# Other priorities for the list schedule of a routed two-part feed-forward stage

## The chip, the core and the metric

The kernel runs on one core of a Trainium2 chip. The metric is the device time of one execution in microseconds (us); lower is better. Times "before" are three runs of the kernel, and one further execution was profiled.

## The reference, cut to what matters

Attention with a feature map comes first, then a routing that gives every one of 8 experts 576 of the 4608 tokens, then two matrix products per expert, then a third and a fourth product that all tokens share:

```
def _moe_ref(x, w_gate, w1, w2):
    ...
    for e in range(E):                        # E = 8, 576 tokens each
        mask = assigned == e
        h = np.maximum(x[mask] @ w1[e], 0.0)  # 512 -> 1024
        out[mask] = h @ w2[e]                 # 1024 -> 512
    ...
def _moe2_ref(x, w_in, w_out):
    h = x @ w_in                              # 512 -> 2048
    g = h - np.tanh(h)
    return (g @ w_out)                        # 2048 -> 512
```

Tokens are assigned greedily: the expert that fills next is found by counting, so the routing of expert p+1 needs the result of expert p.

## The kernel before, in words

The kernel has two parts. `attention` is the first and lasts about a third of the time. `ffn` is the second, and only its order is at stake here. Float32 products are made of three float16 products (high times high, high times low, low times high), so each operand has a high and a low half.

**The planner.** Each part records its operations in a `Sched` object: engine, an estimated duration, what is read and written, and a priority (a smaller number goes first). `run` then plays the engines forward with the estimated durations. Whenever an engine comes free it takes, of the operations whose inputs are ready at that moment, the one with the smallest priority; it waits for nothing that isn't ready unless that is far more urgent. What comes out is one fixed order of instructions for each engine. On the chip every engine works through its order strictly, and waits at an instruction whose inputs are late.

```
            while pend[e] and pend[e][0][0] <= t:
                i = heapq.heappop(pend[e])[1]
                heapq.heappush(avail[e], (self.ops[i][4], i))
```

**The stages of one expert p**, with `TE[p] = 136 p` as the base of its priorities:

- `xt(p)`: five gathers of token rows (GpSimd, L1161), a scaled high half (ScalarE, L1179), a low half (VectorE, L1180), and a transposing DMA on SyncE's queue (L1183). The row buffers `xg` are two, the half buffers `xs` one, so the five rounds follow one another. Priority `TE[p] - 30`.
- `wprep(p)`: gathers of the expert's w1 and w2 (GpSimd, L1097), squares for a norm (ScalarE, L309), high halves (ScalarE, L1118) and low halves (VectorE, L1119). For w1 the priority is `TBT[p-1] + w1`, for w2 `TBT[p-1] + w2`, with `TBT[p] = TE[p] + tb`.
- `g1(p)` and `g2(p)`: 16 and 8 groups of matmuls with 288 columns (L1190, into `mm`), three PSUM banks. After each group of g1 come a relu (ScalarE, L1203, tile `r`), a high half (ScalarE, L1204) and a low half (GpSimd, L1205, tile `xh`); after each group of g2 a high half (L1216) and a low half (VectorE, L1217, tile `gw`).
- `scale_g(p)`: norms of the result (L1233, L1237) and a scale.
- `batch(p)`: 512 of the expert's tokens through the third and fourth product in 16 tiles f. A tile is 12 matmuls of 512 columns into an `mm` bank (L1190), five ScalarE and five VectorE operations for h - tanh(h) (L1315 to L1336, the last two the halves of `gw`), and 12 matmuls of 512 columns that add to four `po` banks (L1342). Up to five tiles of `gw` can stand finished. At the end each `po` bank is copied out (ScalarE, L1353) and scattered to the output rows (GpSimd, L1357). `batch(8)` does the same for the 64 remaining tokens of all experts.
- `routing(p+1)`: sixteen counting steps (VectorE L898, ScalarE L896, a count column on VectorE L846, a small matmul L902 into `rtp`, a comparison on VectorE L904), then the list of rows (L981, L988, `idx` at L992). Priority `TE[p] + route`; its matmuls have at most priority 0, which puts them ahead of nearly all others. The planner treats them as ready `late` us later than their inputs (for p over 0).

The priorities inside `batch`, all from the table `FT`:

```
            for f in range(16):
                tf = T0 + FT["step"] * f
                S.pri = tf
...
                S.pri = tf + FT["sq"]
...
                S.pri = tf + FT["dv"]
...
                S.pri = tf + FT["dv2"]
...
            S.pri = T0 + FT["step"] * 16 + FT["ev"]
```

Here `T0` is `TBT[p]`. The first product of tile f has `tf`; square, tanh and the two functions after the square have `tf` plus `sq`, `th`, `sq2`; the four VectorE steps `dv` and `dv2`; the halves `gh`; the fourth product `lag`; the copies out `ev`. The entry `h` is read nowhere.

Of the kernel before, what the change touches and what calls it, by code (L numbers as in the profile page):

```python
# [38 lines left out]
NW = 96  # L39
MS = 2.0 ** -12  # L40

FT = {'expert': 136.0, 'step': 5.3, 'lag': 11.0, 'route': 5.0, 'xt': -30.0, 'g1': 3.0, 'g2': 24.0, 'g2s': 6.0, 'sg': 49.0, 'tb': 50.0, 'w1': 30.0, 'w2': 40.0, 'rest': 10.0, 'ev': 8.0, 'tb8': 85.0, 'sq': 1.0, 'th': 1.2, 'sq2': 1.1, 'dv': 1.0, 'dv2': 2.0, 'gh': 3.0, 'h': 0.0, 'late': 1.2, 'room': 0.0}
AT = {'hd': -201.4, 'lag': 3.4, 'prep': -30.4, 'load': 19.8, 'proj': -53.9, 'expk': -22.7, 'sub': -13.1, 'expq': -137.2, 'kv': 2.1, 'num': -13.8, 'div': -82.9, 'fin': -101.4, 'conv': 81.9, 'hi': -25.5, 'lo': 83.2, 'tr': 27.2, 'vp': -0.0, 'qproj': 40.6, 'max': 11.5, 'mt': -5.3, 'sqx': -36.8, 'gate': 32.2, 'land': 2.6, 'room': 0.0}
CW = 512
XPE = {0}
# [236 lines left out]
class Kernel:  # L282
# [535 lines left out]
    def routing(self, p, after=()):  # L818
# [33 lines left out]

        late = 1e3 * FT["late"] if p else 0.0

# [164 lines left out]
    def ffn(self):  # L1019
# [3 lines left out]
        pps = ctx.enter_context(tc.tile_pool(name="psf", bufs=1, space=PSUM))  # L1023
        S = self.S = Sched(tc, ports=True, room=1e3 * FT["room"])
        v, act, gp = nc.vector, nc.scalar.activation, nc.gpsimd
# [39 lines left out]

        TE = [FT["expert"] * p for p in range(E)]
        TBT = [t + FT["tb"] for t in TE]
        TBT.append(TBT[-1] + FT["tb8"])

# [12 lines left out]
        def wprep(p, *pri):  # L1082
# [3 lines left out]
            for n, wf in enumerate((w1f, w2f)):  # L1086
# [6 lines left out]
                for c in range(4):  # L1093
                    for b in range(1 + n):
# [10 lines left out]
                S.pe(60, lambda sb=sb: nc.tensor.matmul(self.rtp[:, 508:512], self.onesb, sb, start=False, stop=True, skip_group_check=True), [kss + str(c) for c in range(4)], ["norm"],  # L1105
                     room=1e3 * FT["late"] if p else 0.0)
                S.dve(4, lambda ss=ss: v.tensor_reduce(ss[:, 6:7], self.rtp[:, 508:512], axis=AX.X, op=OP.add), ["norm"], [kss])
# [305 lines left out]
```

## Time and profile before

| | us |
|---|---|
| three runs: median (lowest to highest) | 1783.58 (1779.04 to 1784.16) |
| the profiled execution | 1777.59 |
| its span, first to last instruction | 1775.8 |
| TensorE busy | 1638.1 (92%) |
| VectorE, ScalarE, GpSimd busy | 1333.1, 1270.8, 515.9 |

PE is TensorE's matmuls, PEld its weight loads, DVE VectorE, ACT ScalarE, POOL GpSimd, SP SyncE. A granted clock of 1.00 is 2.4 GHz and 0.50 is 1.2 GHz; a value between is a mean over a stretch at both. The second part has its first expert matmul at 566 us and its last matmul ends at 1758 us.

### The profile page before, as it was taken

What the parts mean: (1) busy time and instruction counts of PE and PEld (TensorE: products, weight loads), DVE (VectorE), ACT (ScalarE), POOL (GpSimd) and SP (SyncE); (2) the same over time, 40 slices, a digit from 0 to 9 for tenths busy, and PEclk for the clock granted to TensorE, in tenths of its full rate; (3) what the DMA queues carried; (4) which work ended last, traced back from release to release, by engine and by line L of the source; (5) the groups of instructions that cost most, each with busy time, mean ns of one, the idle gap of its engine ahead of it and who ended that gap; (6) DMA issues with size and microseconds to landing.
All of it is one profiled execution on the core that took longest, in us unless ns stands there. A gap on an engine that the chain in (4) does not pass through costs nothing. (4 is left out here: it accounts for less than half of the span.)

```text
span 1775.8 us, 32280 instructions
## 1 busy us (share of the span) xinstructions
PE 1638.1 (92%) x11448; PEld 1066.1 (60%) x11448; DVE 1333.1 (75%) x4118; ACT 1270.8 (72%) x2513; POOL 515.9 (29%) x559
## 2 busy tenths in 40 slices
PE   6899999999935999999999999999999999999995
PEld 5888888888822744754754654664664664564442
DVE  6778888778878499589589689689679548436784
ACT  7787889877775679678678668668758658546653
POOL 3332245423043434432332332322322430210000
PEclk9999999889966999999999999999999999999998
DMA  8778776765503022022022022022113250000000
GB/s 202 171 183 190 185 168 153 160 169 142 140 19 115 11 84 63 28 84 69 25 84 65 25 79 71 28 67 76 32 61 83 63 107 13 25 1 1 18 7 24
DMA packets 230419, 145.95 MB, mean 82 GB/s; under 512 B 166080, under 2 KB 208960, under 8 KB 230256
## 3 DMA queue, kind: packets, MB, share of 16 engines
q1 hardware_dynamic: 214208, 90.25, 22.3%
q0 software_dynamic: 16048, 53.62, 9.4%
q8 instruction: 90, 1.47, 0.3%
q14 instruction: 73, 0.60, 0.1%
HBM read 89.16 MB, written 18.87 MB: 61 GB/s over the span
## 5 line engine op out<-in xcount | busy, mean ns | idle before, releaser
L1342 PE MATMUL po<-wout,gw 128*128 128x512 f16 x1728 | 401.3, 380 | 7.6 <-DVE gw L1336 3.9
L1190 PE MATMUL mm<-xh,wt 128*128 128x288 f16 x3072 | 392.2, 288 | 17.2 <-ACT r L1203 10.9
L1190 PE MATMUL mm<-gw,win 128*128 128x512 f16 x1728 | 397.2, 379 | 5.5 <-DVE gw L1217 3.0
L1190 PEld LDWEIGHTS <-wt 128*128 128x128 f16 x3072 | 296.1, 99 | 103.1 <-issue 17.4
L1342 PEld LDWEIGHTS <-gw 128*128 128x128 f16 x1728 | 164.3, 98 | 205.4 <-DVE gw L1336 11.4
L1190 PEld LDWEIGHTS <-win 128*128 128x128 f16 x1728 | 166.0, 98 | 199.3 <-issue 8.2
L1097 POOL DMA_INDIRECT wt<-moe_w,wrow x96 | 125.8, 1310 | 288.9 <-issue 148.4
L544 PE MATMUL bKV<-vp,kp 128*128 128x96 f32 (+1 forms) x1152 | 173.6, 290 | 3.6 <-ACT kvs L551 3.6
L570 PE MATMUL bN<-kvs,qt 128*128 128x96 f32 (+1 forms) x1152 | 158.1, 285 | 5.1 <-ACT qt L527 3.1
L1205 POOL TENSOR_TENSOR xh<-r,xh 128x288 f16<-128x288 f32 x128 | 95.7, 758 | 215.2 <-ACT xh L1204 214.1
L544 PEld LDWEIGHTS bKV<-vp,kp 128*128 128x128 f32 x1152 | 148.2, 197 | 12.9 <-POOL vp L450 4.2
L570 PEld LDWEIGHTS bN<-kvs,qt 128*128 128x128 f32 x1152 | 144.9, 198 | 8.3 <-ACT qt L527 3.3
L1335 ACT ACTIVATE gw<-s,sc 128x512 f16<-128x512 f32 x128 | 91.9, 718 | 53.4 <-DVE s L1328 46.3
L1315 ACT ACTIVATE u<-mm,sc 128x512 f32<-128x512 f32 x128 | 87.0, 679 | 58.4 <-PE mm L1190 57.4
L1336 DVE SCALAR_TENSOR_TENSOR gw<-s,sc,gw 128x512 f16<-128x512 f32 x128 | 98.1, 766 | 18.9 <-ACT gw L1335 18.4
L1324 DVE SCALAR_TENSOR_TENSOR u<-mm,sc,u 128x512 f32<-128x512 f32 x128 | 94.5, 741 | 20.2 <-ACT t L1316 17.2
L1328 DVE COPY_PREDICATED s<-mk,t 128x512 f32<-128x512 uint16 x144 | 105.5, 733 | 0.9
L1317 ACT ACTIVATE s<-u,cst 128x512 f32<-128x512 f32 x144 | 102.9, 714 | 1.3 <-DVE gw L1336 1.2
L1318 ACT ACTIVATE mk<-u,cst 128x512 f16<-128x512 f32 x144 | 102.4, 711 | 0.0
L1327 DVE SCALAR_TENSOR_TENSOR s<-s,u 128x512 f32<-128x512 f32 x144 | 99.9, 694 | 0.8
L904 DVE TENSOR_SCALAR_CACHE_REDUCE r_nn<-rtp,r_rem 128x7 f32<-128x7 f32 x112 | 24.9, 223 | 96.6 <-PE rtp L902 96.5
L1325 DVE SCALAR_TENSOR_TENSOR t<-mm,sc,t 128x512 f32<-128x512 f32 x128 | 94.7, 740 | 2.5 <-ACT t L1316 2.4
(312 smaller groups left out, 2905.6 us busy)
## 6 DMA issues: line engine op xcount, KB each, us to landing
rawk<-k SPq DMA_DIRECT2D x32, 256.0 KB, 3.5
rawv<-v SPq DMA_DIRECT2D x32, 256.0 KB, 3.5
gw<-moe_w_in SPq DMA_DIRECT2D x32, 256.0 KB, 3.2
gw<-moe_w_out SPq DMA_DIRECT2D x32, 256.0 KB, 3.1
rawq<-q SPq DMA_DIRECT2D x30, 256.0 KB, 3.9
xd<-X SPq DMA_DIRECT2D x32, 192.0 KB, 2.6
xd<-X SPq DMA_DIRECT2D x32, 64.0 KB, 2.4
wt<-moe_w,wrow POOLq DMA_INDIRECT x96, 4.2
```

Source lines behind the costliest of these rows:

```text
L544: mm(o, kp[:, c, a * NF:(a + 1) * NF], r, start=sl == 0 and a == 0, stop=sl == 8 and a == 1, skip_group_check=True)
L570: mm(o, qt[:, a, c], r, start=a == 0, stop=a == 1, skip_group_check=True)
L1097: S.pool(1040, lambda dst=dst, col=col, wf=wf: gp.indirect_dma_start(out=dst, out_offset=None, in_=wf, in_offset=bass.IndirectOffsetOnAxis ...
L1190: nc.tensor.matmul(pt.t[:, 0:un], wt(a, d), xs[hl][:, d, u0:u0 + un], start=d == 0 and a == 0 and hl == 0, stop=d == nb - 1 and a == 1)
L1205: S.pool(700, lambda r=r, f=f, u0=u0, un=un: gp.tensor_tensor(hl[:, f, u0:u0 + un], r, hh[:, f, u0:u0 + un], OP.subtract), [kr, f"h.{f}h{u ...
L1317: S.act(512, lambda u=u, s_=s_: act(s_, u, AF.Square, bias=cst[:, 0:1], scale=PC ** 0.5), [ku, "pa"], [ks], pri=tf + FT["sq2"])
L1318: S.act(512, lambda u=u, mk=mk: act(mk, u, AF.Relu, bias=cst[:, 8:9], scale=1024.0), [ku, "t2"], [km], pri=tf + FT["sq2"])
L1325: S.dve_s(512, lambda t=t, pt=pt, sc=sc: v.scalar_tensor_tensor(t, pt.t, sc[:, 0:1], t, op0=OP.mult, op1=OP.subtract), [pt, ksc, kt], [kt])
L1327: S.dve(512, lambda s_=s_, u=u: v.scalar_tensor_tensor(s_, s_, PC * PB, u, op0=OP.add, op1=OP.mult), [ks, ku], [ks], port=True)
L1328: S.dve(512, lambda s_=s_, mk=mk, t=t: v.copy_predicated(s_, mk.bitcast(U16), t), [ks, km, kt], [ks], port=True)
L1336: S.dve_s(512, lambda s_=s_, g=g, sc=sc: v.scalar_tensor_tensor(g[:, 1], s_, sc[:, 2:3], g[:, 0], op0=OP.mult, op1=OP.subtract), [ks, kgr ...
L1342: nc.tensor.matmul(outs[t].t, g[:, a, 128 * t:128 * t + 128], self.wout[:, w, f, :], start=f == 0 and k_ == 0, stop=f == 15 and k_ == 2)
```

## The change

Sixteen numbers of the table `FT` are replaced, fifteen of which are read. No operation is added, removed or altered, and no estimated duration either; only the planner's order of the second part comes out otherwise.

```
-FT = {'expert': 136.0, 'step': 5.3, 'lag': 11.0, 'route': 5.0, 'xt': -30.0, 'g1': 3.0, 'g2': 24.0, 'g2s': 6.0, 'sg': 49.0, 'tb': 50.0, 'w1': 30.0, 'w2': 40.0, 'rest': 10.0, 'ev': 8.0, 'tb8': 85.0, 'sq': 1.0, 'th': 1.2, 'sq2': 1.1, 'dv': 1.0, 'dv2': 2.0, 'gh': 3.0, 'h': 0.0, 'late': 1.2, 'room': 0.0}
+FT = {'expert': 136.0, 'step': 1.8, 'lag': 12.4, 'route': 5.0, 'xt': -30.0, 'g1': 2.5, 'g2': 21.1, 'g2s': 5.2, 'sg': 46.4, 'tb': 53.6, 'w1': 30.0, 'w2': 40.0, 'rest': 27.4, 'ev': -1.8, 'tb8': 64.6, 'sq': 1.0, 'th': 25.4, 'sq2': 3.4, 'dv': 20.9, 'dv2': 2.0, 'gh': 3.4, 'h': -3.3, 'late': 0.6, 'room': 0.0}
```

## Rows read from the trace of the kernel before

**Rows 1.** The page: span, TensorE's busy share, granted clock in 40 slices.

```profile
span 1775.8 us, 32280 instructions
...
PE 1638.1 (92%) x11448; PEld 1066.1 (60%) x11448; DVE 1333.1 (75%) x4118; ACT 1270.8 (72%) x2513; POOL 515.9 (29%) x559
...
PEclk9999999889966999999999999999999999999998
```

**Rows 2.** Busy us of each engine in stretches of 20 us (instructions), clock, DMA.

```profile
940.00:960.00 20.00, 20.00 (x94) 9.11 (x93) 20.00 (x31) 17.67 (x28) 6.48 (x5) 1.00 0.33 79
...
1020.00:1040.00 20.00, 19.11 (x158) 14.84 (x157) 11.92 (x62) 8.40 (x22) 0.00 (x0) 1.00 0.00 1
...
1740.00:1760.00 20.00, 15.72 (x70) 6.30 (x68) 13.29 (x20) 8.31 (x14) 0.97 (x1) 1.00 0.04 14
```

**Rows 3.** What TensorE waited for, 600 to 1760 us: total, times, longest.

```profile
PE mm L1190 <- ACT r L1203: 6.6, 9, 2.0
PE mm L1190 <- DVE gw L1217: 5.4, 7, 2.4
PE po L1342 <- DVE gw L1336: 3.9, 8, 1.5
PE po L1342 <- ACT gw L1332: 2.2, 2, 1.7
PE mm L1190 <- DVE u L1324: 2.0, 1, 2.0
...
PE po L1342 <- ACT gw L1353: 0.6, 1, 0.6
...
PE po L1342 <- ACT gw L1335: 0.5, 2, 0.3
PE mm L1190 <- DVE t L1325: 0.5, 1, 0.5
PE rtp L902 <- DVE r_cnt L846: 0.4, 1, 0.4
```

**Rows 4.** The columns of rows 2, two stretches of 4 us.

```profile
708.00:712.00 4.00, 3.56 (x17) 1.87 (x16) 4.00 (x6) 4.00 (x7) 2.19 (x2) 0.72 0.16 28
...
1440.00:1444.00 4.00, 4.00 (x21) 2.60 (x20) 0.75 (x2) 2.34 (x6) 0.00 (x0) 0.58 0.44 98
```

**Rows 5.** VectorE's groups during one batch, 902 to 988 us: busy us, mean ns.

```profile
L1119 DVE SCALAR_TENSOR_TENSOR wt<-wt,sc 128x1024 f16<-128x1024 f32 x8 | 10.2, 1276 | 0.0
L1180 DVE SCALAR_TENSOR_TENSOR xs<-xg,cst,xs 128x512 f16<-128x512 f32 (+1 forms) x5 | 3.7, 738 | 0.0
```

**Rows 6.** Timeline of routing (start, us, [idle before <- releaser]), three places.

```profile
934.80 1.18 POOL L1161 DMA_INDIRECT xg<-xd,idx  x1 [8.48 <-DVE idx L992]
...
1021.25 0.15 DVE L846 TENSOR_SCALAR r_cnt<-r_ac 128x1 f16<-128x1 f32 x1
...
1023.00 0.17 PE L902 MATMUL rtp<-r_cnt,c 128*128 128x7 f16 x1
...
1274.46 0.17 PE L902 MATMUL rtp<-r_cnt,c 128*128 128x7 f16 x1 [0.45 <-DVE r_cnt L846]
```

**Rows 7.** Timeline of the conversions of token rows, two places.

```profile
973.91 0.74 DVE L1180 SCALAR_TENSOR_TENSOR xs<-xg,cst,xs 64x512 f16<-64x512 f32 x1
...
1437.24 0.72 ACT L1179 ACTIVATE xs<-xg,cst 128x512 f16<-128x512 f32 x1 [4.98 <-DMA xh<-xs]
```

**Rows 8.** Timeline after the last scatter of batch 7.

```profile
1550.02 0.97 POOL L1357 DMA_INDIRECT out<-gw,idx  x1 [2.50 <-DMA out<-gw,idx]
...
1551.78 0.41 ACT L1203 ACTIVATE r<-mm 128x288 f32<-128x288 f32 x1 [3.43 <-POOL xh L1205]
...
1552.24 2.04 PE L1190 MATMUL mm<-xh,wt 128*128 128x288 f16 x12 [1.99 <-ACT r L1203]
```

**Rows 9.** Timeline of TensorE's last matmuls.

```profile
1755.16 3.06 PE L1342 MATMUL po<-wout,gw 128*128 128x512 f16 x12 [1.74 <-ACT gw L1332]
```

## The prediction

> **What bounds the kernel now.** I read the page first, then the stretches of 20 us over the second part, then TensorE's waits, and only then single places in the timeline. TensorE is busy for 92% of the span [rows 1], but the page cannot say whether a busy TensorE is at its peak. The stretches can: in the middle of a batch 94 matmuls pass in 20 us, 0.213 us each [rows 2], and 512 columns at 2.4 GHz are 512/2.4 = 0.213 us. There the array has no hidden room. So TensorE bounds the second part, its work is fixed by the instructions, and a new order can only win back waits, clock lost after waits, and something at the end. The nine waits shown sum to 6.6 + 5.4 + 3.9 + 2.2 + 2.0 + 0.6 + 0.5 + 0.5 + 0.4 = 22.1 us [rows 3]. To them come stretches in which the granted clock fell: 0.72 for 4 us and 0.58 for 4 us, each after a wait [rows 4]. At 0.58 of full speed 4 us do 2.3 us of work, so 1.7 us are lost; at 0.72 it is 1.1 us. The room is thus about 25 us, 1.4% of the time, and a gain beyond it is excluded for the part after 600 us. Before that only `g1`'s own step and `late` differ, and I cost the ramp at nothing: its cover is that routing 0 and the first weights keep their priorities. If ramp orders shift anyway, I allow 2 us either way.
>
> VectorE is the second engine to watch: full, 20.00 of 20, in mid-batch, but 11.92 of 20 while the next expert's second product runs [rows 2]. TensorE is then starved at the end of a batch not because there is too much VectorE work in a cycle, but because too much of it falls into the batch.
>
> **The change part by part.**
>
> *Batch against preparation.* Before, the operations of tile f sit at 5.3 f, so from the sixth tile on the w1 conversion (30) outranks them, from the eighth w2 (40), and from the eleventh the token rows (`TE[p+1]` - 30, which is 56 behind `T0`). Now the first product, square, both functions and the halves lie at 1.8 f to 1.8 f + 3.4, ahead of nearly all preparation; tanh (1.8 f + 25.4) and `dv` (1.8 f + 20.9) fall behind w1 from tiles 3 and 6, behind w2 from tiles 9 and 11, and never behind the token rows (52.4, against at most 52.4). Since each tile needs `dv`, w1 keeps about its place, w2 moves back by two or three tiles, the token rows to the end or into gaps. That is 10.2/2 = 5.1 us of w2 work and 3.7 us of token work [rows 5] that stand less in the way of the late tiles. The waits it aims at are those of batch ends: 3.9 + 2.0 + 0.5 + 0.5 = 6.9 us [rows 3] and 1.1 us of clock [rows 4]. Bounds: 0, if the total of VectorE's work before the batch's end stays what it is, and 8.0 if all go. I take 5 us, nearer to all, because of the next part.
>
> *`late` from 1.2 to 0.6.* Each counting step has one matmul that the planner now places 0.6 us earlier. One step shows it: the count ends at 1021.40 and the matmul starts at 1023.00, 1.60 us later [rows 6]. Sixteen steps would end 16 x 0.6 = 10 us sooner, and so would the list and the first gather, now at 934.80, 32 us into the batch [rows 6]. VectorE's list work then falls partly into the half-empty stretch before the batch, and the token rows start earlier. The gain is counted above. The price: of 1.60 us, 1.0 is left, and where it is less than 0.6 TensorE waits. This happens today once, for 0.45 us [rows 6]; in all 0.4 us [rows 3]. Bounds over seven routings of 16 steps: 0, and 7 x 16 x 0.6 = 67 us if every step lost the whole 0.6. By the shown step nearly all cost nothing; I take 2 us of loss.
>
> The Trainium skill (TensorE: Matmul & The Clock Gate, Part 3, The mechanism) says that matmuls start and end strictly in program order, while only weight loads are pulled ahead. By that rule a routing matmul placed too early holds up every matmul behind it, and its shortfall is paid in full; the upper bound just given is what the sum would rise by. The row of 1274.46 agrees, its wait being TensorE idle time; no row shows more than one such wait.
>
> *First product before fourth.* Before, fourth products (`lag` 11.0) alternate with first ones from tile f - 2; now all first products outrank them (12.4 is 6.9 tiles), so TensorE runs ahead as far as three banks allow. Inside a batch this costs nothing: TensorE has the other product to do, and up to five finished tiles can wait. If that cover went, a batch would lose one bank's turn, a 2.6 us tile. In the last batch it pays: the last tile starts sooner, while fourth products are still in hand, and the wait of 1.74 us before the last twelve matmuls [rows 9], one of 2.2 us in all [rows 3], shrinks. Bounds 0 and 2.2; I take 1.5. The chain of scatters behind is not altered.
>
> *Copies out (`ev`) and the mixed batch.* They move ahead of the mixed batch's first tiles, which removes the 0.6 us [rows 3]; taken as 0.5.
>
> *g1, g2, sg, rest.* Their spacing shrinks, but inside these stages nearly nothing competes. The waits for the first product of a batch (5.4 us, seven times [rows 3]) are six of about half a us, the path from the last group's bank through ScalarE and VectorE, and I leave those. The seventh, 2.4 us, follows a ScalarE instruction that stood 4.98 us waiting for a transposing DMA [rows 7] with a copy-out of g2 behind it, and 1.7 us of clock were lost after it [rows 4]: 4.1 us that hang on where the token rows stand in ScalarE's order. Bounds 0 and 4.1; taken as 2.
>
> *What stays.* The 6.6 us behind relus [rows 3]. In the place shown, GpSimd waits 2.50 us at the fourth scatter for the third one's landing, the subtraction of g1 queues behind it, the relu waits 3.43 us for a free tile and TensorE 1.99 us [rows 8]. No priority here shortens a landing.
>
> **Sum.** -5 + 2 - 1.5 - 0.5 - 2 = -7 us; in the profile's own time 1777.6 - 7 = 1770.6 us. That execution is 6.0 us below the median of the three, so against the median the forecast is 1783.6 - 7 = 1776.6 us, rounded to 1776.5.
>
> **The rivals.**
>
> *A: the waits move but do not go.* VectorE does the same work per cycle, and if routing ends no sooner on the chip, the batch still ends with VectorE full; the first five us fall away. The sum is then +2 - 1.5 - 0.5 - 2 = -2: 1781.5 us. For it: VectorE full at 20.00. Against: 8 us idle in the stretch before [rows 2]. That the new order is nearly the old one ends at the same time.
>
> *B: slower, through the routing matmuls.* If the lead time in the plan is used up by real delays, half of the 112 steps may lose 0.3 us: 17 us instead of 2, and the sum is -7 + 15 = +8: 1791.5 us. It decides from a mean loss of (7 + 2)/112 = 0.08 us per step on. For it: the one wait of 0.45 us. Against: 1.60 us in the shown step.
>
> *C: the scatter waits go too,* because copies out come at other moments against g1: a further -6.6, and with it 1770 us. Nothing in the rows speaks for it but that their times depend on the order.
>
> A late last token row is no rival of weight: the last of five is converted at 973.91 [rows 7], about 15 us before the batch's fourth products end, and only half of each g1 group needs the last two.
>
> **How the numbers follow.** A measurement of this kernel tells about 0.3%, 5.4 us, from no change; the three runs span 5.1 us (the table above). Forecast 0.48 (own range -3 to -14 us; 0.39 of it beyond 5.4), A 0.27 (0.25 within, 0.02 faster), B 0.18 (0.15 slower, 0.03 within), C 0.07 (faster). Faster 0.48, same 0.37, slower 0.15. The range reaches from the room nearly used up, 1783.6 - 19 = 1765, to somewhat short of B, 1789; beyond lie some 0.08 on either side.
>
> **What would show it.** Right: fewer waits for `gw` and `u` at batch ends, first gathers about 10 us earlier in the batch, VectorE below 20.00 late in the batch, a shorter wait before the last twelve matmuls, relu waits as before. Wrong: waits at L902 and L988 of several us (B), or the list of waits with the same 20 us under other lines (A), or a preparation that is late, with g1 waiting for `xh` or `wt`.

## The result, and the profile after

The changed kernel takes 1794.40 us (median of 4 runs, 1790.94 to 1797.47) against 1782.92 us of the kernel before (4 runs): a ratio of 1.0062, 95% interval 1.0034 to 1.0089. It is slower, by about 11 us, where 7 us of gain were forecast. The profiled execution took 1790.94 us.

The page and the stretches of 20 us of the changed kernel, with the columns of [rows 1] and [rows 2]:

```profile
span 1789.2 us, 32383 instructions
...
PE 1638.3 (92%) x11448; PEld 1065.8 (60%) x11448; DVE 1333.1 (75%) x4118; ACT 1264.9 (71%) x2513; POOL 486.4 (27%) x559
...
PEclk8999999889966999999999999999999999999998
```

```profile
960.00:980.00 20.00, 20.00 (x96) 9.04 (x95) 18.54 (x44) 14.97 (x27) 0.90 (x1) 1.00 0.19 38
980.00:1000.00 20.00, 20.00 (x117) 10.64 (x116) 13.98 (x69) 7.40 (x17) 1.01 (x1) 1.00 0.05 17
1000.00:1020.00 20.00, 14.56 (x117) 10.96 (x115) 8.06 (x29) 13.12 (x33) 11.10 (x14) 1.00 0.10 41
```

TensorE's busy time is the same to 0.2 us, so the 13.4 us of longer span are waiting. The batch itself has become what the change aims at: TensorE 20.00 of 20 to its end, with VectorE no longer full. But the 20 us right behind it, where the next expert's g1 begins, have TensorE idle for 5.4 us, and no other engine is full there either: everybody waits for somebody.

What TensorE waited for from 600 us to its end (compare [rows 3]):

```profile
PE mm L1190 <- ACT r L1203: 23.3, 15, 2.9
PE rtp L902 <- DVE r_cnt L846: 4.7, 5, 2.7
PE mm L1190 <- POOL wt L1116: 3.5, 1, 3.5
PE mm L1190 <- DVE gw L1217: 2.5, 5, 0.8
PE rtp L988 <- DVE r_buf L981: 1.5, 1, 1.5
...
PE mm L1190 <- DVE t L1325: 0.8, 3, 0.3
```

The lines for `po` and for `u`, 9 us in [rows 3], are gone. In their place the waits behind relus have risen from 6.6 to 23.3 us. The timeline of one such place, the start of g1 of expert 3, on GpSimd, on ScalarE and on TensorE:

```profile
1000.25 0.99 POOL L1357 DMA_INDIRECT out<-gw,idx  x1 [4.75 <-ACT gw L1353]
1003.70 0.97 POOL L1357 DMA_INDIRECT out<-gw,idx  x1 [2.47 <-issue]
1007.28 0.97 POOL L1357 DMA_INDIRECT out<-gw,idx  x1 [2.61 <-DMA out<-gw,idx]
1008.28 1.42 POOL L1205 TENSOR_TENSOR xh<-r,xh 128x288 f16<-128x288 f32 x2
```

```profile
999.54 0.69 ACT L1353 ACTIVATE gw<-po,sc 128x512 f32<-128x512 f32 x1 [0.94 <-DMA out<-gw,idx]
1003.03 0.69 ACT L1353 ACTIVATE gw<-po,sc 128x512 f32<-128x512 f32 x1 [2.80 <-DMA out<-gw,idx]
...
1003.95 0.40 ACT L1203 ACTIVATE r<-mm 128x288 f32<-128x288 f32 x1
...
1009.05 0.41 ACT L1203 ACTIVATE r<-mm 128x288 f32<-128x288 f32 x1 [3.03 <-POOL xh L1205]
```

```profile
1004.40 3.30 PE L1190 MATMUL mm<-xh,wt 128*128 128x288 f16 x24 [2.90 <-ACT r L1203]
1009.51 0.77 PE L1190 MATMUL mm<-xh,wt 128*128 128x288 f16 x5 [1.81 <-ACT r L1203]
```

From issue to landing of all scatters:

```profile
DMA to landing us min/median/max: 2.7/2.8/5.0
```

Read them together. The last three scatters stand 3.5 us apart, since GpSimd holds each until the one before has landed: the first three land at 999.46, 1002.95 and 1006.52 us in the trace, and the next ones start 0.7 to 0.8 us behind. What holds them are the program's own semaphore waits on the scatters' line, for these landings; no run took the wait away with the scatters kept. The planner's entry for a scatter is 1.04 us of GpSimd and no tie between scatters, so it put all four ahead of g1's first subtraction. Not one subtraction runs until 1008.28, the three `r` tiles stay full, and the relu of 1009.05 waits 3.03 us. The copies out suffer from the same spacing: with two `ob` buffers the fourth waits 2.80 us on ScalarE for a landing, and the relus queue behind it. TensorE, with three banks, pays 2.90 and 1.81 us. The place of [rows 8] is the same knot with 1.99 us.

GpSimd at the same g1 in the kernel before, where subtractions (L1205) run ahead of the scatters and between them:

```profile
991.89 0.73 POOL L1205 TENSOR_TENSOR xh<-r,xh 128x288 f16<-128x288 f32 x1 [0.74 <-ACT xh L1204]
993.12 1.02 POOL L1357 DMA_INDIRECT out<-gw,idx  x1 [0.50 <-ACT gw L1353]
996.65 0.99 POOL L1357 DMA_INDIRECT out<-gw,idx  x1 [2.50 <-ACT xh L1204]
997.66 0.74 POOL L1205 TENSOR_TENSOR xh<-r,xh 128x288 f16<-128x288 f32 x1
...
1003.72 0.99 POOL L1357 DMA_INDIRECT out<-gw,idx  x1 [1.84 <-ACT r_jk L896]
```

### The profile page after: what moved, and what is told of

Same layout as the page of the kernel before. It is cut to its first block, busy times and chain, and to the rows that moved or that the text cites. A ratio compares the mean times of both kernels' runs of the same rounds, so it can differ in the third digit from the quotient of the medians.

```text
span 1789.2 us, 32383 instructions
## 1 busy us (share of the span) xinstructions
PE 1638.3 (92%) x11448; PEld 1065.8 (60%) x11448; DVE 1333.1 (75%) x4118; ACT 1264.9 (71%) x2513; POOL 486.4 (27%) x559
## 5 line engine op out<-in xcount | busy, mean ns | idle before, releaser
L1190 PE MATMUL mm<-xh,wt 128*128 128x288 f16 x3072 | 399.0, 290 | 31.0 <-ACT r L1203 24.1
L1190 PE MATMUL mm<-gw,win 128*128 128x512 f16 x1728 | 391.4, 379 | 2.8 <-DVE gw L1217 1.7
L1342 PE MATMUL po<-wout,gw 128*128 128x512 f16 x1728 | 390.2, 379 | 0.0
L1190 PEld LDWEIGHTS <-wt 128*128 128x128 f16 x3072 | 294.5, 99 | 122.0 <-issue 37.8
L1190 PEld LDWEIGHTS <-win 128*128 128x128 f16 x1728 | 167.2, 98 | 202.6 <-issue 5.7
L1097 POOL DMA_INDIRECT wt<-moe_w,wrow x96 | 102.0, 1063 | 177.5 <-DVE wt L1119 62.9
L1357 POOL DMA_INDIRECT out<-gw,idx x32 | 33.1, 1036 | 418.8 <-ACT gw L1353 373.2
L1317 ACT ACTIVATE s<-u,cst 128x512 f32<-128x512 f32 x144 | 104.1, 723 | 10.5 <-DVE gw L1333 8.9
L1205 POOL TENSOR_TENSOR xh<-r,xh 128x288 f16<-128x288 f32 x128 | 97.5, 776 | 42.5 <-ACT xh L1204 41.7
```

The costliest lines, as they stand in the source:

```text
L1097: S.pool(1040, lambda dst=dst, col=col, wf=wf: gp.indirect_dma_start(out=dst, out_offset=None, in_=wf, in_offset=bass.IndirectOffsetOnAxis ...
L1190: nc.tensor.matmul(pt.t[:, 0:un], wt(a, d), xs[hl][:, d, u0:u0 + un], start=d == 0 and a == 0 and hl == 0, stop=d == nb - 1 and a == 1)
L1205: S.pool(700, lambda r=r, f=f, u0=u0, un=un: gp.tensor_tensor(hl[:, f, u0:u0 + un], r, hh[:, f, u0:u0 + un], OP.subtract), [kr, f"h.{f}h{u ...
L1317: S.act(512, lambda u=u, s_=s_: act(s_, u, AF.Square, bias=cst[:, 0:1], scale=PC ** 0.5), [ku, "pa"], [ks], pri=tf + FT["sq2"])
L1342: nc.tensor.matmul(outs[t].t, g[:, a, 128 * t:128 * t + 128], self.wout[:, w, f, :], start=f == 0 and k_ == 0, stop=f == 15 and k_ == 2)
```

## The experiments

Besides the ratio to the kernel before on the same chip I give the **stretch** from the first g1 matmul (L1190) to the end of TensorE's last matmul in the profiled execution: 1191.8 us before, 1204.6 changed. It leaves out the first part, which no edit touches and which ended anywhere from 566 to 587 us in these executions. A stretch is one execution: its difference to before lies up to 7 us from what the ratio says, so smaller differences of stretch alone show nothing. **Relu waits** of the whole stretch are 10.9 us before and 24.1 changed; 4.3 us of those before stand in the first expert, ahead of 600 us. Three theories stand against each other, spelled out in the first two expectations: S (the scatters and copies out), P (the batch's priorities, which make g1 dense) and L (`late`). Runs are called e1 to e12 by their numbers here.

**1. Copies out where they were.**

```
-'ev': -1.8   +'ev': 60.4     (the changed kernel; 142.8 behind TE[p], as before)
```

> The changed kernel with ev set to 60.4, so that the copies out of the fourth product's banks stand where they stood before against the next expert's relus (142.8 behind the expert's base). Theory S (the copies out and the four scatters, each of which waits for the landing of the one before, block ScalarE and GpSimd at the start of g1): the wait of the first product behind relus falls from 23 us to below 14 and the time by 8 us or more, to about 1785. Theory P (the batch's own priorities end it in one block of fourth products, so that g1 starts dense behind it and meets the same scatters anyway): the wait stays above 18 us and the time within 4 us of the changed kernel. Theory L (late): no change.

Ratio 1.0090 (1.0058 to 1.0122), stretch 1204.3. The waits did what theory S said, the time did not:

```profile
PE mm L1190 <- ACT r L1203: 6.1, 10, 1.1
PE rtp L902 <- DVE r_cnt L846: 5.5, 2, 2.9
PE mm L1237 <- ACT s L1233: 3.9, 4, 2.3
PE mm L1190 <- DVE t L1325: 3.8, 5, 2.6
```

18 us of relu waits went, and about 14 came elsewhere over the stretch: behind `u`, `t`, the norm's squares and the routing's list. So `ev` moves the knot; putting it back undoes the waits but is no cure in this order.

**2. `late` back.**

```
-'late': 0.6   +'late': 1.2   (the changed kernel)
```

> The changed kernel with late back at 1.2. Theory L (routing matmuls placed too early make TensorE wait and move the chain of relus): the waits at L902 and L988 fall from 7 us to about 1, and the time by 6 us or more. Theories S and P: those waits are mostly a knock-on of ScalarE standing still before the counting step, they stay above 3 us, and the time moves by less than 3 us.

Ratio 1.0250 (1.0201 to 1.0300), stretch 1231.3: far slower, which no theory had expected. Relu waits stayed at 23.5 us; waits behind `u` and `t` rose to 11.9 us, and the mean granted clock over the stretch fell to 0.984 from 0.992, which is (1 - 0.984) x 2 x 1231 = 39 us at the lower level instead of 20. The list of rows came 30 us after the batch's start again (963.6 against a first product at 932.8, for expert 3), as before, where the changed kernel has it 5 us ahead of it (906.8 against 911.7). Theory L falls for the changed kernel: with its priorities the smaller `late` is a help.

**3 and 4. The planner is told that scatters follow one another.**

```
-S.pool(1040, ... scatter(ob, it), [ko] + kit, [], lat=2500)
+S.pool(1040, ... scatter(ob, it), [ko] + kit, ["out"], lat=2500)
```

No instruction changes; the plan now spaces scatters by 3.7 us. On the changed kernel:

> The changed kernel, with one thing told to the planner: every scatter follows the one before it (it writes the key out), so that the plan holds 3.7 us between scatters instead of 1.04 us. No instruction changes, only the order that comes out. Theory S: GpSimd's subtractions of g1 are now placed between the scatters, the relu waits fall below 10 us and the time by 12 us or more, to 1782 or lower. Theory P: the g1 groups still arrive dense, the waits stay above 15 us, the gain is below 6 us. Theory L: no change.

Ratio 0.9987 (0.9964 to 1.0010), stretch 1187.2. Against the changed kernel's 1.0062 that is 0.75%, 13 us, and 17.4 us of stretch. What TensorE waited for:

```profile
PE rtp L902 <- DVE r_cnt L846: 5.3, 3, 2.6
PE rtp L988 <- DVE r_buf L981: 3.4, 6, 1.3
PE mm L1190 <- issue: 3.3, 2, 3.0
PE mm L1190 <- ACT r L1203: 3.2, 4, 1.2
```

The relu waits fell from 23.3 to 3.2 us as theory S has it: three to seven of g1's subtractions now run between the first and the fourth scatter of batches 0 to 6, where the changed kernel has one in two of them and none in five. On the kernel before:

> The kernel before with the same key for the scatters. Theory S: its relu waits of 6.6 us fall to 2 to 3 us and the time by 2 to 6 us, to about 1779. Theories P and L: within 2 us of before.

Ratio 0.9978 (0.9953 to 1.0004), a gain of 4 us that is not clear of nothing, and stretch 1181.3, 10.5 us shorter; the only relu wait left is the one of the first expert, which slipped behind 600 us because its first part ended later:

```profile
PE mm L1190 <- DVE gw L1217: 5.2, 7, 2.2
PE mm L1190 <- ACT r L1203: 4.3, 1, 4.3
PE po L1342 <- DVE gw L1336: 3.9, 8, 1.5
```

With the scatters planned, then, the sixteen numbers gain nothing over those before either: ratio 0.9987 against 0.9978, stretch 1187.2 against 1181.3.

**5 and 6. The same orders without the scatters.** The planner sees the scatters, but the 32 of batches 0 to 7 are not issued.

```
-lambda ob=ob, it=it: scatter(ob, it)
+lambda ob=ob, it=it: scatter(ob, it) if mix else None
```

> The changed kernel in the same order, with the 32 scatters of batches 0 to 7 left out (those rows of the output are not written); only the mixed batch still scatters. Theory S: with nothing to wait for on GpSimd and no landing before a copy out, the relu waits fall from 23 us to below 4 and the stretch from the first g1 matmul to TensorE's end from 1204.6 to about 1183 us, 1.2% less. Theory P: g1's density alone overruns ScalarE's relus and conversions, the waits stay above 12 us and the stretch above 1193 us.

> The kernel before in its own order, with the same 32 scatters left out. Theory S: it loses only the 6.6 us of relu waits and what hangs on them, so its stretch falls from 1191.8 to about 1183 us, half of what the changed kernel gains. Theory P: within 3 us of 1191.8.

Changed kernel: ratio 0.9872 (0.9828 to 0.9915), stretch 1167.3. Kernel before: 0.9932 (0.9905 to 0.9958), stretch 1182.7. In the same order, then, the scatters cost the changed kernel 37.3 us, more than the 21.6 us that theory S expected, and the kernel before 9.1 us as expected. This is the whole of a scatter, its issue on GpSimd and its transfer with the wait for its landing; the two runs do not separate these. All of TensorE's waits after 600 us fall from 38.9 to 10.1 us in the changed kernel. Of the changed kernel's waits this is left:

```profile
PE rtp L902 <- DVE r_cnt L846: 2.9, 2, 2.7
PE mm L1190 <- DVE gw L1217: 1.7, 4, 0.5
...
PE mm L1190 <- ACT r L1203: 1.2, 2, 0.9
```

Theory P, that a dense g1 overruns ScalarE by itself, falls. And without scatters the new priorities are the better ones, by 1182.7 - 1167.3 = 15.4 us.

**7. `late` alone.**

```
-'late': 1.2   +'late': 0.6   (the kernel before)
```

> The kernel before with late 0.6 alone. If late is what brings the list of rows forward, the first gather of token rows comes about 30 us earlier against the batch's start than now, as in the changed kernel. Theory L: it costs: waits at L902 and L988 rise from 1 us to 6 or more, time up by 5 us or more. Theory S: it is a gain or nothing, waits at the batch's end (6.9 us) shrink, time between -8 and 0 us.

Ratio 1.0043 (1.0023 to 1.0064), stretch 1197.2. The list of rows came 17 to 46 us sooner against the batches of experts 0 to 5 (930.5, 5 us behind the first product, for expert 3), and waits behind `gw` at batch ends fell (3.9 to 1.5), but waits at L902 rose from 0.4 to 6.8 us and those at L988 to 2.3 us, and relu waits to 12.4. In the order of before, theory L holds for the time and the waits at L902 and L988; how the loss divides between these and the relu waits is not shown.

**8. Early copies out alone.**

```
-'ev': 8.0   +'ev': -54.2     (the kernel before; 80.6 behind TE[p], as changed)
```

> The kernel before with its copies out as early as in the changed kernel (ev -54.2, which puts them at 80.6 behind the expert's base), nothing else. Theory S in its narrow form (the early copies out are the cause): relu waits rise from 6.6 us to 12 or more and the time by 5 us or more. Theory S in its wide form (it is the dense g1 behind the batch that meets the scatters, whatever ev is): waits within 3 us of 6.6, time within 4 us.

Ratio 1.0050 (1.0025 to 1.0074), stretch 1200.0. Relu waits 17.5 us in the whole stretch against 10.9, and ScalarE stood 17.1 us in front of copies out waiting for landings, against 13.5. The narrow form of theory S holds here.

**9 to 11. What is left when the scatters are planned.**

```
e3 with 'late': 1.2 | e4 with 'late': 0.6 | e3 with 'late': 0.9
```

> The changed kernel with the scatters' chain told to the planner and late back at 1.2: what is left is the batch's own priorities. Theory S: relu waits stay below 6 us, since the scatters are planned; waits at L902 and L988 fall from 10 us to about 2. If late 0.6 was a loss beside that, the stretch from the first g1 matmul to TensorE's end falls from 1187 to about 1180 us. Rival (late 0.6 is needed with these priorities, because the token rows are late without it, as the run with late 1.2 and unplanned scatters suggests): the stretch rises above 1192 us, with waits for VectorE's u and t.

> The kernel before with the scatters' chain told to the planner and late 0.6. With the scatters planned, late alone should no longer raise the relu waits (12.4 us where they were not planned): below 5 us. Theory L: waits at L902 and L988 stay 5 us or more above those of late 1.2, and the stretch is 3 us or more above the 1181 us without it. Rival: the earlier list of rows pays more than it costs at batch ends, and the stretch is 1178 us or less.

> The changed kernel with the scatters' chain told to the planner and late 0.9, halfway. A candidate for a version faster than both: routing waits of about 4 us instead of 10, relu waits below 6 us, stretch about 1180 us, time about 0.5% below before. If the order that the planner finds is as sensitive as the other runs suggest, anything between 1178 and 1195 us.

The first: 0.9980 (0.9949 to 1.0012), stretch 1188.5. Relu waits are 8.6 us, two waits of 4.3, both behind ScalarE's w2 conversions (L1114, L1115) of the first two experts and none behind a scatter, and L902 hardly waits; within 1.3 us of `late` 0.6, so with planned scatters these two values of `late` make no measured difference to these priorities. Theory S had expected relu waits below 6 us and a stretch of about 1180 us, the rival above 1192 us; neither came. The second: 1.0055 (1.0024 to 1.0085), stretch 1205.4. Relu waits 1.2 us, but routing matmuls that stood too early:

```profile
PE rtp L988 <- DVE wo L981: 6.6, 1, 6.6
PE mm L1190 <- DVE t L1325: 5.9, 3, 4.7
PE rtp L988 <- DVE r_buf L981: 4.6, 3, 2.1
```

A list matmul held TensorE for 6.6 us once. The Trainium skill (TensorE: Matmul & The Clock Gate, Part 3, The mechanism) has matmuls run strictly in program order; this wait, idle time with expert matmuls queued behind it, agrees. The third: 0.9946 (0.9915 to 0.9976), stretch 1186.1, with 2.4 us of relu waits; the time is the one expected, the stretch is longer than the 1180 us of the candidate.

**12. Early copies out with planned scatters.**

```
e4 with 'ev': -54.2
```

> The kernel before with its copies out early (ev -54.2), which alone brought the relu waits from 10.9 to 17.5 us over the whole second part, and now with the scatters' chain told to the planner. Theory S: early copies out are harmless once the plan holds the scatters apart: relu waits at or below 5 us (4.3 of them stand at the first expert and have another cause), stretch within 4 us of 1181 us, time 0.4 to 0.8% below the run with early copies out alone. Rival (early copies out delay the relus by their own ScalarE time): relu waits stay above 9 us and the stretch above 1190 us.

Ratio 0.9951 (0.9932 to 0.9970), median 1775.34 us, stretch 1178.7, the shortest of all that scatter. The time is 1.0% below the run with early copies out alone, where 0.4 to 0.8 were expected. Relu waits are 4.3 us, the one in the first expert:

```profile
PE po L1342 <- DVE gw L1336: 4.4, 9, 1.5
PE mm L1190 <- ACT r L1203: 4.3, 1, 4.3
```

The same early copies out that cost 0.50% cost nothing once the plan knows the scatters. This kernel and e11 beat both kernels of the case, by half a per cent against the one before.

## Why the prediction was wrong, by its own steps

**The step that failed is "What stays".** It took the 6.6 us behind relus as unchanged, because no priority shortens a landing. It had the knot right, [rows 8], and missed that the cost is not the landing but what is queued behind it, which order decides. In the order of before, g1's first groups run among the last fourth products, at each of batches 0 to 6 two or three subtractions are done before the first scatter and one to three more before the last, and TensorE waits 0.3 to 2.2 us behind relus. In the new order the fourth products come first; g1 starts dense, no subtraction precedes the first scatter, and each of the seven places costs 2.6 to 4.9 us. These places are the whole sum: 6.6 us became 23.3. That the scatters are the cause is shown by e5 and e6 (37.3 against 9.1 us in unchanged orders) and by e3 (relu waits down to 3.2 by one planner key). Which of the new numbers brings it about is not one alone: early copies out do it in the order of before (e8), but taking them back does not mend the new one in time (e1). Two parts of the prediction lead to this place and were priced elsewhere: `ev` moves the copies out of every batch, from 142.8 to 80.6 behind the expert's base, and was costed for the mixed batch alone; "First product before fourth" asked what the new order does inside a batch and in the last one, not what meets g1 behind it.

**Rival C had the right place and the wrong sign:** scatters and copies out did come at other moments against g1. I gave it 0.07, for a gain only.

**Batch against preparation was right.** The 6.9 us at batch ends went to 0.8, more than the 5 taken; VectorE is no longer full late in the batch (18.54 and 13.98 of 20).

**`late` was right in direction and mis-sized.** The first gather moved from 32 us behind the batch's first product to 4.5 us ahead of it, not by 10 us but by 37:

```profile
907.21 0.96 POOL L1161 DMA_INDIRECT xg<-xd,idx  x1 [2.25 <-DVE idx L992]
```

With `late` back (e2) or alone (e7) the whole shift goes or comes, so it is `late`'s. The routing of expert 1 shows what I left out. Its first count stands at 570.4 us in both traces and its sixteenth at 637.3 before and 626.1 changed, 11 us sooner, as forecast; the matmuls from there to the list, which have the same `late`, give 6 us more (`idx` at 671.4 and 654.0). The rest adds up from expert to expert, since each routing needs the one before: the first count for expert 3 comes at 800.9 us instead of 846.1, and the shift against the batch grows from 17 us for expert 1 to 45 for expert 6. My bound counted seven routings of 16 steps; `late` acts on the counts of six, since the first routing has none and the last does not count: 96 steps, 58 us for them at most instead of 67, and 14 us instead of 17 in rival B. Its price, taken as 2 us, is 4.3 + 1.6 = 5.9 us at L902 and L988. Of the 4.7 us at L902, 1.8 hang on the scatters (2.9 remain in e5). In the order of before, `late` alone is a loss of 0.43% (e7).

**First product before fourth, and `ev` at the mixed batch, were right:** the 2.2 us before the last matmuls and the 0.6 us are gone. TensorE ends in one block of 84 matmuls without a wait:

```profile
1753.12 18.29 PE L1342 MATMUL po<-wout,gw 128*128 128x512 f16 x84
```

**The seventh wait for `gw`** fell from 2.4 us to 0.8 at most, more than the half that was taken.

**The wins and the losses:** waits that shrank give -6.1 (batch ends), -2.4 (tail), -0.6, -2.9 (`gw`), together -12.0; those that grew +16.7 (relus), +4.3 and +1.6 (routing), +3.5, together +26.1. The difference of 14 us is close to the 13.4 us of longer span. The +3.5 is one wait at g1 of expert 1 for a w1 half that GpSimd makes (L1116): deferred preparation that came late, named as a sign of failure, not priced.

**Open:** why the changed kernel with `late` 1.2 loses 2% more while its scatters are unplanned (e2) and nothing when they are planned (e9). The trace shows where, but no run separates the causes. Open too is what the 3.5 us between scatters would be without the wait for the landing.

## What to carry to other kernels

Before searching priorities, compare each planned gap with the traced one: a search tunes the order to the model, and here the model had scatters 1.0 us apart that stand 3.5 us apart. Over the stretch the new numbers were 15 us better than the old without the scatters of batches 0 to 7, 13 us worse with scatters unplanned, and no better with scatters planned. When a list of waits names an in-order queue, ask what an edit will place behind the blocked instruction, not only whether the block gets shorter. One planner key gave back 0.75% where sixteen tuned numbers had lost 0.62%; with it, one number of the table (e12) was enough for a gain of 0.5%.

## What the runs showed of the hardware

Scatters to one output, 128 rows of 512 each, each waiting for the landing of the one before, went out 3.45 to 3.6 us apart in the middle of the changed kernel (1000.25, 1003.70, 1007.28) as at its end, where TensorE had finished (1773.93, 1777.38, 1780.98), and GpSimd did nothing behind a waiting one. TensorE's granted clock was 0.58 over the 4 us from 1440 us on in the kernel before [rows 4], most of that time at 1.2 GHz, behind a wait of 2.35 us; it was 0.72 over the 4 us from 708 us on [rows 4], behind waits of 0.26 and 1.54 us. These are the two longer waits, from the kernel before:

```profile
706.08 3.77 PE L1342 MATMUL po<-wout,gw 128*128 128x512 f16 x10 [1.54 <-DVE gw L1336]
...
1439.84 6.37 PE L1190 MATMUL mm<-xh,wt 128*128 128x288 f16 x37 [2.35 <-DVE gw L1217]
```

In the changed kernel it was 0.83 on average over the 20 us from 740 us on, at whose start a wait of 2.74 us at L902 ended and one of 0.88 us followed:

```profile
740.00:760.00 20.00, 18.76 (x135) 14.10 (x135) 10.75 (x62) 11.37 (x29) 10.38 (x9) 0.83 0.00 1
```
